# Batch 0's keys and queries in 2 KB runs, two heads stacked on the partitions, and the first batch's steps in another order

## The chip, the core and the metric

The kernel runs on one core of a Trainium2 chip. The metric is the device time of one execution in microseconds. Before the change the median of three runs is 712.56 us (711.0 to 712.8). The engines are called as in the profile: PE (TensorE, matrix products), DVE (VectorE), ACT (ScalarE), POOL (GpSimd) and SP (SyncE, whose instruction stream here only issues DMA transfers). Each engine works through its own instructions in order and waits at an instruction until what it needs is there.

## What is computed

Two attentions, one behind the other, and a gated feed-forward layer on their result. There are 8 batches of 8 heads, 576 tokens and a head size of 64; 32 rows of p attend to all tokens, and then all tokens attend to the 32 packed rows.

```python
def sm_attn(qq, kk, vv):
    s = scale * np.matmul(qq, kk.transpose(0, 1, 3, 2))
    s = s - np.max(s, axis=-1, keepdims=True)
    a = np.exp(s)
    a = a / (np.sum(a, axis=-1, keepdims=True) + 1e-09)
    return np.matmul(a, vv)
p_packed = sm_attn(p, k, v)
out = sm_attn(q, p_packed, p_packed)
...
x = np.ascontiguousarray(attn_out.transpose(0, 2, 1, 3)).reshape(B * S, H * D)
a = x @ w_a
b = x @ w_b
return (a * b @ w_out).astype(np.float32)
```

x has 4608 rows of 512, w_a and w_b are 512 by 1536, w_out is 1536 by 512. All is float32.

## The kernel before

**Stages.** The packed rows of a batch are multiplied into w_a and w_b (the small products g, line 380), so that a batch's feed-forward input is an attention matrix of 576 tokens by 256 (8 heads by 32 packed rows). A first product makes a and b from it (`mm1`, line 398, in float32r halves "hi" and "lo", three products for each pair), DVE multiplies them, and a second product with w_out (line 424 for batch 0, line 738 later) gives the output. Twelve tiles `ft` of 128 columns cover the 1536. Batches 0 and 1 run in this plain form, batches 2 to 7 in a loop of periods with fewer products (line 779), which the change doesn't touch.

**Attention steps.** For a batch, `stage1(b, e)` handles the four heads of one parity e ("head set e"): scores of p against k (line 264), maximum (270), exp (282), transposes (300), product with v (310). `stage2(b, e)` does the second attention: scores (325), transposition out of PSUM (330), maximum (334), subtraction (337), exp (339), sum (343 to 345), multiplication (346), transposition (350), and the halves a2_hi and a2_lo (356, 91). Subtraction and multiplication run on DVE or POOL by the letter in the string SUBS. Each stage is a generator that is moved on by one step whenever its name stands in a list: S0 and S1 start stage 1 for set 0 and 1, r0 and r1 move it on, s0 and s1 move stage 2 on, P turns the packed rows, T turns p, k and q turn tiles of keys and queries, Lk, Lq, Lv and Lp issue loads.

**Weights.** Each block of w_a, w_b and w_out is loaded as two 32-bit words for each number (`raw`, lines 216 and 223). Step A works on the high words (line 195, ACT), B on the low words (ACT line 203, DVE or POOL line 200, by the string WAYS), C combines them into `w_ab` (line 206, DVE); D splits a block of w_out.

**The order by hand.** All five engines run in the order in which the code emits instructions. FIRST is the order of batch 0's loads, all on SP's queue; up to eight transfers are in flight, and the ninth is issued when the first has landed. START is the order of batch 0's attention steps, weight steps and fillers (W, nine products that only keep TensorE going, line 567) until the first feed-forward product. PLAN_0 has a slot for each half tile of batch 0's first product and for each of the first nine f of its second product; its steps belong to batch 1's attention (with their own loads for batches 1 and 2) and to the weights. TURN says which engine copies each transposed tile out of PSUM.

**Batch 0's loads.** `load_first` (line 131) loads k and q each as two transfers of 512 KB, heads 0 to 3 and heads 4 to 7. A partition holds four tokens of each of four heads, in runs of 4 by 64 numbers, 1 KB; a third transfer (128 KB, 32 partitions) brings the last 64 tokens. `turn_first` (line 145) transposes four 128 by 128 blocks for each pair of heads and copies them out of PSUM as one block of 512 columns. `load_v` (line 164) loads v for one head set in one transfer for the first 512 tokens and two small ones for the rest. `store_first` (line 442) writes batch 0's rows back in the token order that the loads set.

Of the kernel before, what the change touches and what calls it, by code (L numbers as in the profile page):

```python
# [8 lines left out]
F32 = mybir.dt.float32  # L9
# [10 lines left out]
def tile_packed_attn_gated_ffn(  # L20
# [20 lines left out]
    nc = tc.nc  # L41
    B, H, S, D = q.shape
# [3 lines left out]
    P = 128  # L46
    R, E = 4, 2
# [24 lines left out]
    scratch = early.__enter__()  # L72
# [3 lines left out]
    ident = const.tile([P, P], F32, name="ident")  # L76
# [28 lines left out]
    nats, xTs = {}, {}  # L105
# [23 lines left out]
    firsts = {}  # L129

    def load_first(src, key, part):

        if part < 2:
            t = scratch.tile([P, R, 4 * D], F32, name=f"{key}n{part}")
            nc.sync.dma_start(
                out=t, in_=src[0, R * part:R * part + R, 0:4 * P, :].rearrange("h (p i) d -> p h (i d)", i=4))
        else:
            t = scratch.tile([P, H, 2 * D], F32, name=f"{key}n{part}")
            nc.sync.dma_start(out=t[0:TR], in_=src[0, :, 4 * P:S, :].rearrange("h (p u) d -> p h (u d)", u=2))
        firsts[key, part] = t  # L140

    def turn_first(key, n):

        if (0, key) not in xTs:
            pool = scratch if key == "q" else ld
            xTs[0, key] = [pool.tile([P, R, HS], F32, name=f"xT{i}") for i in range(2)]
        copy = (nc.vector.tensor_copy, nc.scalar.copy)[int(TURN["kq".index(key) * 5 + n])]
        x = bank_pair()[:, 0, :] if n in (2, 3) else bank()
        if n < 4:
            h = 2 * (n % 2)  # L150
            for i in range(4):
                nc.tensor.transpose(
                    x[:, P * i:P * i + P], firsts[key, n // 2][:, h + i // 2, P * (i % 2):P * (i % 2) + P], ident)
            copy(out=xTs[0, key][n // 2][:, h:h + 2, 0:2 * P], in_=x.rearrange("p (h t) -> p h t", h=2))
# [8 lines left out]
    def load_v(b, e):  # L163


        t = ld.tile([P, R, NT, D], F32, name="vt") if b or e == 0 else scratch.tile([P, R, NT, D], F32, name="vt1")
        vv = v[b].rearrange("(r e) s d -> e s r d", e=E)[e]
        n = 2 if b else 4
        for i in range(4 // n):
            nc.sync.dma_start(  # L170
                out=t[:, :, n * i:n * i + n, :].rearrange("p r u d -> p r (u d)"),
                in_=vv[n * P * i:n * P * i + n * P].rearrange("(p u) r d -> p r u d", u=n).rearrange("p r u d -> p r (u d)"))
        for u in range(2):
            nc.sync.dma_start(
                out=t[TR * u:TR * u + TR, :, 4, :],
                in_=vv[4 * P:S].rearrange("(p u) r d -> u p r d", u=2)[u])
        vts[b, e] = t
# [19 lines left out]
    def low_word(raw, way):  # L197
        low = raw[..., 0]
        if way:
            (nc.vector if way == 1 else nc.gpsimd).tensor_scalar(  # L200
                out=low, in0=low, scalar1=2.0 ** -29, scalar2=7.0, op0=ALU.mult, op1=ALU.min)
        else:
            nc.scalar.activation(out=low, in_=low, func=AF.Copy, scale=0.93 * 2.0 ** -29)
# [115 lines left out]
    def stage2(b, e):  # L319
# [15 lines left out]
        yield  # L335
        eng = nc.vector if b < 2 and SUBS[2 * b + e] == "1" else nc.gpsimd
        eng.tensor_tensor(out=s2, in0=s2, in1=mx.unsqueeze(2).broadcast_to([P, TU, J]), op=ALU.subtract)
# [104 lines left out]
    def store_first(ob, x, i):  # L442

        for u in range(2):
            if x < 8:
                rows = out[0:4 * P].rearrange("(a l i) n -> a i l n", a=4, i=4)[x % 4, 2 * (x // 4) + u]
            else:
                rows = out[4 * P:S].rearrange("(l u) n -> u l n", u=2)[u]
            nc.sync.dma_start(out=rows, in_=ob[i + TL * u:i + TL * u + TL])
# [55 lines left out]

    st = {}

    FIRST = ("k0 p0 k2 k1 q0 v0 q1 v1 q2 w1 w1 w1 w1 w1 w1 w1 w1 w1 w1 w1")
    START = ("T0 k0 k4 k1 k3 k2 q0 S0 S1 r0 r1 q1 r1 r0 r0 r1 r0 q2 r1 q3 q4 P0 s0 B s1 W A s0 B A A s0 s0 B s1 C A s1 B s0 C s1 A s1 C B B Lp2 C A B A s0 s1 B C B B s0 B g A C A A s1 Lk2 C C A A C B B Lk3 C s1")
    WAYS = ("000000022220202120012012011200010010")  # L510
    TURN = ("0001110101")
    SUBS = ("0100")

    PLAN = (" |  |  | S0 | r0 | r0 |  | r0 |  | r0 Lv1 ; S1 | r1 | r1 q0 Lk2 | r1 | r1 | q1 Lk3 Lv2 P0 |  ; s0 | s0 s0 | s0 T2 | "
            "s0 Lp4 | s0 s1 | s1 s1 | s1 | s1 | s1 | t0 t1 t2 t3 u0 | k2 |  | k3 Lq2")
    PLAN = dict(enumerate(PLAN.split("|")))
    PLAN_0 = ("A | C C | B A B A | B C C B C | A A | C | B Lv0 | C B A T0 k0 Lp2 A | A A B B C Lq0 | C C k1 | A B A | S0 B | B A r0 | C C C | B A Lq1 |  | C C B r0 r0 D A A | S1 C D | B C B B A D | r1 C | A A D | r0 T2 |  | q0 B r1 C B D r1 C |  | A | D B C Lv1 A | r1 A B D Lk2 B C B q1 D Lk3 A A P0 | C s0 s0 D C Lp4 A B | s1 s0 | Lv2 | D | s0 s1 s0 | k2 s0 s1 C k3 | s1 |  | Lq2 D s0 s1 s1 Lq3 s1")
    PLAN_0 = dict(enumerate(PLAN_0.split("|")))

    pieces = [(c, n) for c in range(NC) for n in range(4)] + [(NC, f) for f in range(NFT)]  # L520
# [12 lines left out]
    def convert(x):  # L533
# [62 lines left out]
    emit(0, START, tasks)
    drain(tasks["g"])
# [316 lines left out]
    for n in range(LAST):  # L914
        b, ft = NB + n // NFT, n % NFT
# [18 lines left out]
    i, c0 = tiles[-1]  # L934
# [35 lines left out]
```

## Time and profile before

| | us |
|---|---|
| median of three runs | 712.56 |
| lowest and highest run | 711.0, 712.8 |
| span of the profiled execution, first to last instruction | 710.5 |
| TensorE busy in that span | 700.2 |
| DVE, ACT, POOL busy | 452.7, 363.6, 416.2 |
| first product of line 398 starts | 32.29 |

The profiled execution is known by its span alone; the lowest of the timed runs is 0.5 us longer and the median 2.06 us. The granted TensorE clock is 1.000. Times in the trace are counted from the first instruction. A row of the timeline gives start and length in us, engine, line, operation, tiles written and read, size and count, and in brackets how long the engine had been idle before and what ended that. A matrix product in float32 appears as two instructions. In the table by stretches the last two columns are the share of time in which the 16 DMA engines were busy (slightly over 1 when all are) and the GB/s that they moved.

### The profile page before, as it was taken

The page shows a single profiled execution, that of the slowest core. Times are in us where ns is not written, and L with a number is a line of the kernel's source. Part 1 is how long each engine was busy: PE and PEld are TensorE (multiplying, and loading weights), DVE is VectorE, ACT ScalarE, POOL GpSimd, SP SyncE. Part 2 cuts the span into 40 slices and gives each one's busy share as a digit, 9 for nine tenths or more (in the row PEclk, how much of TensorE's full clock was granted, in tenths as well). Part 3 has the DMA queues.
Part 4 walks back from the last instruction along what each step waited for, and adds up shares of the span by engine and source line. Part 5 has one row for each costly group of instructions (what it writes and reads, how often), then busy time and mean ns, then how long its engine had stood idle before and what let it go on. Part 6 is the DMA issues. An engine that isn't in the chain of part 4 may idle for free.

```text
span 710.5 us, 14214 instructions
## 1 busy us (share of the span) xinstructions
PE 700.2 (99%) x5568; PEld 574.8 (81%) x5568; DVE 452.7 (64%) x820; ACT 363.6 (51%) x733; POOL 416.2 (59%) x322
## 2 busy tenths in 40 slices
PE   8899999999999999999999999999999999999998
PEld 6488978898878888878888788788888878888886
DVE  3998655467355679665775678765785667754342
ACT  3878743544254555645554456545555446544510
POOL 0586752327244677746874589556775578856520
PEclk9999999999999999999999999999999999999999
DMA  9999963668254736446433564456145323133002
GB/s 267 385 249 326 235 138 75 184 155 286 78 127 155 180 85 167 127 134 152 137 95 123 155 177 94 118 181 166 60 120 160 104 90 119 60 121 116 1 1 75
DMA packets 178243, 102.64 MB, mean 144 GB/s; under 512 B 142464, under 2 KB 160640, under 8 KB 172800
## 3 DMA queue, kind: packets, MB, share of 16 engines
q1 hardware_dynamic: 178176, 101.73, 50.4%
q8 instruction: 44, 0.72, 0.4%
q14 instruction: 23, 0.19, 0.1%
HBM read 85.98 MB, written 15.73 MB: 143 GB/s over the span
## 4 chain that ended last, share of the span: by engine, by line
PE 94%; DVE 3%; ACT 1%; DMA 1%; issue 0%; SPq 0%; DVEq 0%; ACTq 0%
PE x L738 37%; PE m L779 29%; PE m L398 10%; PE m L424 5%; PE x L793 5%; PE s L310 2%; PE s L325 1%; PE s L264 1%; PE x L380 1%; PE s L300 1%; DMA qn<-in_q_dram 1%; DVE w_ab L206 1%; DVE a_lo L91 0%; PE x L310 0%; ACT raw L195 0%
## 5 line engine op out<-in xcount | busy, mean ns | idle before, releaser
L738 PE MATMUL x<-wo,h_hi 128*128 128x512 f32 (+1 forms) x776 | 249.2, 391 | 0.0
L91 POOL TENSOR_TENSOR h_lo<-asb,h_hi 128x576 fp32r<-128x576 f32 x96 | 140.6, 1466 | 84.5 <-ACT h_hi L824 44.6
L738 PEld LDWEIGHTS x<-wo,h_hi 128*128 128x128 f32 x776 | 140.9, 188 | 22.0 <-ACT gs L799 0.9
L738 PE MATMUL x<-wo,h_lo 128*128 128x512 f32 (+1 forms) x388 | 152.1, 392 | 0.0
L91 POOL TENSOR_TENSOR G_lo<-gs,G_hi 128x640 fp32r<-128x640 f32 x72 | 112.7, 1571 | 30.5 <-ACT G_hi L814 30.2
L738 PEld LDWEIGHTS x<-wo,h_lo 128*128 128x128 f32 x388 | 72.9, 188 | 11.7
L91 POOL TENSOR_TENSOR A_lo<-gs,A_hi 128x256 fp32r<-128x256 f32 x36 | 27.3, 758 | 89.1 <-ACT A_hi L802 89.1
L861 DVE TENSOR_TENSOR d<-m,d 128x576 f32<-128x576 f32 (+1 forms) x73 | 54.1, 741 | 34.7 <-ACT d L857 34.0
L874 DVE TENSOR_TENSOR asb<-m,d 128x288 f32<-128x288 f32 x72 | 32.5, 451 | 66.1 <-ACT c L870 64.2
L870 ACT COPY c<-m 128x288 f32<-128x288 f32 x72 | 28.8, 399 | 79.2 <-PE m L779 79.2
L748 DVE TENSOR_TENSOR part<-x,part 128x512 f32<-128x512 f32 (+1 forms) x65 | 44.1, 679 | 38.8 <-PE x L738 38.8
L779 PE MATMUL m<-tx_hi,G_hi 128*128 128x288 f32 x216 | 63.8, 296 | 0.0
L779 PE MATMUL m<-tx_hi,G_lo 128*128 128x288 f32 x216 | 63.7, 295 | 0.0
L799 ACT COPY gs<-x 128x512 f32<-128x512 f32 x36 | 21.1, 587 | 82.5 <-PE x L793 81.2
L779 PE MATMUL m<-tx_lo,G_hi 128*128 128x288 f32 x216 | 63.3, 293 | 0.0
L814 ACT CAST G_hi<-gs 128x640 fp32r<-128x640 f32 x72 | 52.2, 729 | 15.8 <-POOL gs L808 15.2
L857 ACT COPY d<-m 128x576 f32<-128x576 f32 (+1 forms) x73 | 46.6, 639 | 19.9 <-PE m L779 18.2
L824 ACT CAST h_hi<-asb 128x576 fp32r<-128x576 f32 x72 | 49.0, 680 | 11.5 <-DVE asb L888 11.5
L779 PEld LDWEIGHTS m<-a_hi,G_hi 128*128 128x128 f32 x144 | 27.0, 187 | 31.5 <-issue 17.4
L808 POOL TENSOR_TENSOR gs<-gs 128x512 f32<-128x512 f32 x36 | 46.6, 1294 | 4.1 <-DVE gs L805 3.7
L779 PE MATMUL m<-a_hi,G_hi 128*128 128x288 f32 x144 | 47.0, 326 | 0.0
L398 PE MATMUL m<-a_hi,ghi 128*128 128x288 f32 x192 | 43.2, 307 | 1.6 <-ACT ghi L386 1.5
(174 smaller groups left out, 1550.9 us busy)
## 6 DMA issues: line engine op xcount, KB each, us to landing
wr<-w_kept SPq DMA_DIRECT2D x36, 1024.0 KB, 5.0
nat<-in_k_dram SPq DMA_DIRECT2D x56, 144.0 KB, 5.2
nat<-in_q_dram SPq DMA_DIRECT2D x56, 144.0 KB, 5.4
vt<-in_v_dram SPq DMA_DIRECT2D x28, 256.0 KB, 3.8
out_dram<-part SPq DMA_DIRECT2D x27, 256.0 KB, 2.0
raw<-in_moe_w_a_dram SPq DMA_DIRECT2D x12, 512.0 KB, 8.6
raw<-in_moe_w_b_dram SPq DMA_DIRECT2D x12, 512.0 KB, 8.8
raw<-in_moe_w_out_dram SPq DMA_DIRECT2D x12, 512.0 KB, 7.0
```

What stands on the lines that cost most here:

```text
L91: return eng.tensor_tensor(out=dst, in0=src, in1=hi.bitcast(F32), op=ALU.subtract)
L398: nc.tensor.matmul(out=ps[:, half, 0:HS], lhsT=gt[:, kt, ft % 4, cols], rhs=at[:, kt, HS * half:HS * half + HS], start=(n == 0 and kt == 0 ...
L424: nc.tensor.matmul(out=o[:, cols], lhsT=ht[:, c0:c0 + P], rhs=wt[:, cols], start=(ft == 0 and n == 0), stop=(ft == NFT - 1 and n == 2))
L738: nc.tensor.matmul(out=o[:, cols], lhsT=ht[:, c0:c0 + P], rhs=wt[:, cols], start=(ft == fts[0] and n == 0), stop=end)
L748: nc.vector.tensor_tensor(out=parts[i][:, cols], in0=o[:, cols], in1=parts[i][:, cols], op=ALU.add)
L779: nc.tensor.matmul(out=bank[:, n % 2, 0:HS], lhsT=g, rhs=t, start=(first and i == 0), stop=(i == 2), skip_group_check=True)
L793: nc.tensor.matmul(out=gps[e][J * r:J * r + J, :], lhsT=ppT[rows, 2 * (b % 2), r, :], rhs=w[rows, r, :], start=True, stop=True)
L808: nc.gpsimd.tensor_tensor(out=gs[:, 2:4].rearrange("p a u f -> p a (u f)"), in0=gs[:, 0:2].rearrange("p a u f -> p a (u f)"), in1=s2.unsqu ...
L814: nc.scalar.copy(out=G_hi[:, n % 3], in_=gs[:, 1:6, n % 2])
L824: nc.scalar.copy(out=view(h_hi[ft]), in_=src)
L857: nc.scalar.copy(out=d[:, both], in_=X[:, both, 0:HS])
L861: nc.vector.tensor_tensor(out=d[:, both], in0=V[:, both, 0:HS], in1=d[:, both], op=ALU.add)
```

## The change

**Loads.** k and q of batch 0 are still loaded in two large transfers each, but now heads 2a and 2a+1 lie under each other: even heads on partitions 0 to 63, odd heads on partitions 64 to 127. A partition holds eight tokens of each of four heads, a run of 8 by 64 numbers, 2 KB. Each transfer thus writes 64 partitions, and both are needed before a block can be transposed, since a block of 128 partitions now holds two heads. v must follow the same token order, so its 512 KB transfer becomes two of 256 KB, one for each half of the partitions, still in 1 KB runs. The copies out of PSUM and the store rows follow. The SP queue takes both k transfers first, q before v, and the end of q before q's second half.

**Orders.** START, WAYS, TURN, SUBS and PLAN_0 are new. In SUBS batch 0's head set 1 goes from DVE to POOL.

On SP, the first transfers of the program (kn and qn are the tiles of k and q, vt those of v, raw the weight blocks). Before:

```order
L135 DMA kn_113<-in_k_dram 128x4x256
L182 DMA p_nat<-in_p_dram 128x2x64 x2
L139 DMA kn_118<-in_k_dram 32x8x128
L135 DMA kn_120<-in_k_dram 128x4x256
L135 DMA qn_122<-in_q_dram 128x4x256
L170 DMA vt<-in_v_dram 128x4x256
L174 DMA vt<-in_v_dram 32x4x64 x2
L135 DMA qn_128<-in_q_dram 128x4x256
L170 DMA vt_130<-in_v_dram 128x4x256
L174 DMA vt_130<-in_v_dram 32x4x64 x2
L139 DMA qn_134<-in_q_dram 32x8x128
L216 DMA raw<-in_moe_w_a_dram 128x2x512 x2
```

And now:

```order
L138 DMA kn_113<-in_k_dram 64x4x512 x2
L190 DMA p_nat<-in_p_dram 128x2x64 x2
L141 DMA kn_119<-in_k_dram 32x8x128
L138 DMA qn_121<-in_q_dram 64x4x512
L141 DMA qn_123<-in_q_dram 32x8x128
L138 DMA qn_121<-in_q_dram 64x4x512
L174 DMA vt<-in_v_dram 64x4x256 x2
L182 DMA vt<-in_v_dram 32x4x64 x2
L174 DMA vt_131<-in_v_dram 64x4x256 x2
L182 DMA vt_131<-in_v_dram 32x4x64 x2
L224 DMA raw<-in_moe_w_a_dram 128x2x512 x2
```

All large transfers of k, q and v are 64 partitions wide, and v comes behind all of q.

On DVE, batch 0's second attention (s2_0 and s2_1 are the scores of head sets 0 and 1, raw_136 to raw_142 the first four weight blocks). Before:

```order
L252 COPY ppT_100<-x_343 128x256
L330 STREAM_TRANSPOSE s2_0_377<-s_347 128x576
L334 TENSOR_REDUCE mx_379<-s2_0_377 128x18
L330 STREAM_TRANSPOSE s2_1_387<-m_357 128x576
L334 TENSOR_REDUCE mx_389<-s2_1_387 128x18
L206 SCALAR_TENSOR_TENSOR w_ab_95<-raw_136 128x2x256
L337 TENSOR_TENSOR s2_1_387<-s2_1_387,mx_389 128x576
L343 TENSOR_REDUCE sum2_399<-s2_0_377 128x18
```

And now:

```order
L260 COPY ppT_100<-x_337 128x256
L156 COPY xT1_232<-m_341 128x2x256
L214 SCALAR_TENSOR_TENSOR w_ab_95<-raw_136 128x2x256
L338 STREAM_TRANSPOSE s2_0_385<-s_348 128x576
L342 TENSOR_REDUCE mx_387<-s2_0_385 128x18
L338 STREAM_TRANSPOSE s2_1_393<-m_361 128x576
L342 TENSOR_REDUCE mx_395<-s2_1_393 128x18
L214 SCALAR_TENSOR_TENSOR w_ab_95<-raw_138 128x2x256
L351 TENSOR_REDUCE sum2_403<-s2_0_385 128x18
```

The subtraction of head set 1 has left DVE (the multiplication too, further on), and the first weight combination and a q copy stand ahead of the score transposes.

On PE, in batch 0's second product, batch 1's value product of head set 1 (wo are the blocks of w_out, one for each f). Before:

```order
L424 MATMUL m_1181<-wo_1080,h_hi3_499 128x512 x2
L424 MATMUL m_1181<-wo_1080,h_lo3_500 128x512
L310 MATMUL s_1243<-vt_1225,t2_1169 32x64 x20
L250 MATMUL x_1291<-ident_90,pp_1120 128x128 x2
L424 MATMUL m_1180<-wo_1166,h_hi4_501 128x512 x2
```

And now:

```order
L432 MATMUL m_1182<-wo_1036,h_hi2_497 128x512 x2
L432 MATMUL m_1182<-wo_1036,h_lo2_498 128x512
L318 MATMUL s_1234<-vt_1228,t2_1169 32x64 x20
L432 MATMUL m_1181<-wo_1079,h_hi3_499 128x512 x2
L432 MATMUL m_1181<-wo_1079,h_lo3_500 128x512
```

The value product stands behind f = 2 instead of f = 3, and the turn of the packed rows (line 250, now 258) no longer follows it at once but comes behind f = 3. On SP the load of p for batch 2 (two transfers) now stands ahead of that v load, where before it stood behind the next eight k transfers.

The diff, without the unchanged lines and with the tables cut to a line or two:

```diff
@@ load_first
         if part < 2:
-            t = scratch.tile([P, R, 4 * D], F32, name=f"{key}n{part}")
-            nc.sync.dma_start(
-                out=t, in_=src[0, R * part:R * part + R, 0:4 * P, :].rearrange("h (p i) d -> p h (i d)", i=4))
+            t = firsts.get((key, 0))
+            if t is None:
+                t = firsts[key, 0] = scratch.tile([P, R, 8 * D], F32, name=f"{key}n0")
+            rows = src[0, :, 0:4 * P, :].rearrange("(a g) (p i) d -> g p a (i d)", g=2, i=8)[part]
+            nc.sync.dma_start(out=t[64 * part:64 * part + 64], in_=rows)
@@ turn_first
             for i in range(4):
-                nc.tensor.transpose(
-                    x[:, P * i:P * i + P], firsts[key, n // 2][:, h + i // 2, P * (i % 2):P * (i % 2) + P], ident)
-            copy(out=xTs[0, key][n // 2][:, h:h + 2, 0:2 * P], in_=x.rearrange("p (h t) -> p h t", h=2))
+                j = 4 * (i % 2) + 2 * (i // 2) if key == "k" else 2 * i
+                nc.tensor.transpose(x[:, P * i:P * i + P], firsts[key, 0][:, n, D * j:D * j + P], ident)
+            copy(
+                out=xTs[0, key][n // 2][:, h:h + 2, 0:2 * P].rearrange("p h (i t) -> p h i t", i=4),
+                in_=x.rearrange("p (i h t) -> p h i t", i=4, h=2))
@@ load_v
-        for i in range(4 // n):
+        for g in range(0 if b else 2):
+            nc.sync.dma_start(
+                out=t[64 * g:64 * g + 64, :, 0:4, :].rearrange("p r u d -> p r (u d)"),
+                in_=vv[0:4 * P].rearrange("(p g u) r d -> g p r u d", g=2, u=4)[g].rearrange("p r u d -> p r (u d)"))
+        for i in range(2 if b else 0):
@@ store_first
-                rows = out[0:4 * P].rearrange("(a l i) n -> a i l n", a=4, i=4)[x % 4, 2 * (x // 4) + u]
+                rows = out[0:4 * P].rearrange("(a l i) n -> a i l n", a=2, i=8)[x % 2, 2 * (x // 2) + u]
@@ tables (START and PLAN_0 are new as well)
-    FIRST = ("k0 p0 k2 k1 q0 v0 q1 v1 q2 w1 w1 w1 w1 w1 w1 w1 w1 w1 w1 w1")
+    FIRST = ("k0 k1 p0 k2 q0 q2 q1 v0 v1 w1 w1 w1 w1 w1 w1 w1 w1 w1 w1 w1")
-    WAYS = ("000000022220202120012012011200010010")
-    TURN = ("0001110101")
-    SUBS = ("0100")
+    WAYS = ("020000022220202120012111011200010010")
+    TURN = ("0000101000")
+    SUBS = ("0000")
```

More of the change, by code (lines that the diff above doesn't have):

```diff
@@ L139, in load_first @@
             nc.sync.dma_start(out=t[0:TR], in_=src[0, :, 4 * P:S, :].rearrange("h (p u) d -> p h (u d)", u=2))
-        firsts[key, part] = t
+            firsts[key, part] = t
     def turn_first(key, n):
@@ L506, in tile_packed_attn_gated_ffn @@
     st = {}
-    FIRST = ("k0 p0 k2 k1 q0 v0 q1 v1 q2 w1 w1 w1 w1 w1 w1 w1 w1 w1 w1 w1")
-    START = ("T0 k0 k4 k1 k3 k2 q0 S0 S1 r0 r1 q1 r1 r0 r0 r1 r0 q2 r1 q3 q4 P0 s0 B s1 W A s0 B A A s0 s0 B s1 C A s1 B s0 C s1 A s1 C B B Lp2 C A B A s0 s1 B C B B s0 B g A C A A s1 Lk2 C C A A C B B Lk3 C s1")
-    WAYS = ("000000022220202120012012011200010010")
-    TURN = ("0001110101")
-    SUBS = ("0100")
+    FIRST = ("k0 k1 p0 k2 q0 q2 q1 v0 v1 w1 w1 w1 w1 w1 w1 w1 w1 w1 w1 w1")
+    START = ("k0 k1 k2 T0 k3 k4 S0 r0 S1 q1 r1 q0 q4 r1 r0 r0 q2 r1 r0 r1 P0 q3 A s0 A B B B s1 W C s0 s0 A s0 B s1 s1 A C s1 s0 B C A s1 B C B B Lp2 A s0 B B A s1 C B s0 A s1 g A C A A B C Lk2 C s1 A C Lk3 C B")
+    WAYS = ("020000022220202120012111011200010010")
+    TURN = ("0000101000")
+    SUBS = ("0000")
     PLAN = (" |  |  | S0 | r0 | r0 |  | r0 |  | r0 Lv1 ; S1 | r1 | r1 q0 Lk2 | r1 | r1 | q1 Lk3 Lv2 P0 |  ; s0 | s0 s0 | s0 T2 | "
@@ L516, in tile_packed_attn_gated_ffn @@
     PLAN = dict(enumerate(PLAN.split("|")))
-    PLAN_0 = ("A | C C | B A B A | B C C B C | A A | C | B Lv0 | C B A T0 k0 Lp2 A | A A B B C Lq0 | C C k1 | A B A | S0 B | B A r0 | C C C | B A Lq1 |  | C C B r0 r0 D A A | S1 C D | B C B B A D | r1 C | A A D | r0 T2 |  | q0 B r1 C B D r1 C |  | A | D B C Lv1 A | r1 A B D Lk2 B C B q1 D Lk3 A A P0 | C s0 s0 D C Lp4 A B | s1 s0 | Lv2 | D | s0 s1 s0 | k2 s0 s1 C k3 | s1 |  | Lq2 D s0 s1 s1 Lq3 s1")
+    PLAN_0 = ("A A B | C | B B | A C | B C C B A A | C | C Lv0 | A C B T0 | k0 Lp2 A Lq0 A A B B C | C C k1 | A B A | | S0 B B C A r0 | C C | B A Lq1 | | C C B r0 r0 D A A | S1 C D | B C B B A D | r1 C | A D | A r0 T2 q0 | B | B r1 C D r1 B C | | Lp4 A | D C Lv1 A r1 | A B Lk2 D B C B q1 D Lk3 A A P0 | C s0 s0 D C | A s1 s0 Lv2 | D s0 B s1 s0 | | k2 | s0 s1 C k3 | s1 | | Lq2 D s0 s1 s1 Lq3 s1")
     PLAN_0 = dict(enumerate(PLAN_0.split("|")))
```

## The prediction

> **What bounds the kernel now.** I read the page first, then a table by stretches, then what TensorE waited for, then the head of the trace instruction by instruction. The page:
>
> ```profile
> span 710.5 us, 14214 instructions
> PE 700.2 (99%) x5568; PEld 574.8 (81%) x5568; DVE 452.7 (64%) x820; ACT 363.6 (51%) x733; POOL 416.2 (59%) x322
> ```
>
> TensorE is busy for all but 10 us. Two rows of the table by stretches say where that rest lies (columns: length, then busy time of PE, PEld, DVE, ACT and POOL, granted clock, DMA share, GB/s):
>
> ```profile
> 20.00:40.00 20.00, 17.62 (x103) 9.62 (x93) 19.76 (x31) 16.11 (x29) 13.45 (x8) 1.00 1.06 380
> 40.00:60.00 20.00, 19.89 (x182) 17.27 (x181) 18.65 (x28) 16.55 (x31) 14.08 (x8) 1.00 0.95 250
> ```
>
> From 40 us on TensorE hardly pauses. From 20 to 40 us DVE is the full engine (19.76 of 20) and the DMA queue is full too (1.06). TensorE's waits, whole program:
>
> ```profile
> PE m L398 <- ACT ghi L386: 1.5, 1, 1.5
> PE s L325 <- DVE ppT L252: 0.6, 1, 0.6
> PE x L380 <- DVE w_ab L206: 0.6, 1, 0.6
> PE x L152 <- DMA qn<-in_q_dram: 0.5, 1, 0.5
> PE x L250 <- DVE pp L316: 0.4, 1, 0.4
> ```
>
> All small. But the head holds more than waits: until the first product of the feed-forward part (L398) starts, TensorE does little that counts, and part of it is filler (L567).
>
> ```profile
> 7.98 1.09 PE L152 MATMUL m<-ident,kn 128*128 128x128 f32 x8
> 15.92 0.96 PE L310 MATMUL x<-vt,a1T 128*32 128x64 f32 x40
> 16.81 0.66 PE L152 MATMUL m<-ident,qn 128*128 128x128 f32 x4
> 19.05 0.72 PE L325 MATMUL s<-xT,ppT 64*32 64x288 f32 x16 [0.61 <-DVE ppT L252]
> 20.19 7.99 PE L567 MATMUL m<-kn,ident 128*128 128x512 f32 x18
> 32.29 0.54 PE L398 MATMUL m<-a_hi,ghi 128*128 128x288 f32 x2 [1.48 <-ACT ghi L386]
> ```
>
> So the end moves with two things: when L398 starts (32.29), and stalls of the in-order TensorE after that. Both are touched here.
>
> **The change part by part: the loads.** The k pair, the q pair and the v pairs are now each written to 64 partitions at a time, one half behind the other on one queue. Before, all large loads wrote 128. What the DMA engines move in each form:
>
> ```profile
> 3.00:4.00 1.00, 1.00 (x4) 0.77 (x3) 0.00 (x0) 0.00 (x0) 0.00 (x0) 1.00 1.08 366
> 4.00:5.00 1.00, 1.00 (x4) 0.82 (x3) 0.00 (x0) 0.00 (x0) 0.00 (x0) 1.00 0.82 185
> 17.00:18.00 1.00, 1.00 (x12) 0.80 (x11) 0.72 (x2) 0.00 (x0) 0.00 (x0) 1.00 1.06 391
> 385.00:385.50 0.50, 0.50 (x6) 0.50 (x5) 0.00 (x0) 0.00 (x0) 0.50 (x1) 1.00 0.95 201
> 385.50:386.00 0.50, 0.50 (x6) 0.50 (x5) 0.00 (x0) 0.10 (x1) 0.50 (x1) 1.00 0.99 217
> 389.00:389.50 0.50, 0.50 (x7) 0.50 (x5) 0.00 (x0) 0.34 (x1) 0.00 (x0) 1.00 1.04 393
> out_dram<-part SPq DMA_DIRECT2D x2, 128.0 KB, 2.3
> ```
>
> At 3 us k goes to 128 partitions in 1 KB runs: 366 GB/s. At 17 us weights go to 128 partitions in 2 KB runs: 391. The change's own words point at that pair of rows: 2 KB runs are worth 7%. But at 385 us two stores of 64 partitions each (128 KB, 2 KB runs, one half behind the other) move 201 and 217 GB/s while the engines are 0.95 and 0.99 busy, and at 389 us one store from 128 partitions moves 393. No load of 64 partitions is in this trace, so the new loads lie between 201 and 391 GB/s; I take 210, as the stores have the same shape, run and queue. [...]
>
> ```profile
> L135 SPq DMA_DIRECT2D kn<-in_k_dram x2: 444/448/453, 0.7 to 3.2; - x2
> DMA to landing us min/median/max: 4.0/4.0/4.7
> 6.52 0.69 DVE L154 COPY xT<-x 128x512 f32<-128x512 f32 x1
> 11.03 0.76 DVE L270 TENSOR_REDUCE nmx<-s 128x1 f32<-128x576 f32 x1 [1.23 <-PE s L264]
> ```
>
> The first k load, 512 KB issued at 0.73, landed in 4.0 us: 1.43 at 366 GB/s, so 2.57 are fixed. The new pair, 1,049 KB at 210 GB/s, takes 5.0 and lands at 0.73 + 2.57 + 5.0 = 8.3. Until now the second half was at hand at 7.98 and the first half's work was done by then. Now every transpose needs both halves, so four copies (0.69 each), p's copy (0.4), the first transposes (0.6) and the score products (0.8) follow 8.3: row maxima (L270) at about 12.9 instead of 11.03, **1.9 us later**. That the score products no longer stand behind the first q load (0.5 of wait, 0.6 of work) is counted in that.
>
> Next is v. Ahead of the last v half lie 3,146 KB in half loads (15.0 us at 210) and 459 KB in small pieces (2.5 us at the 185 of the row at 4 us); it lands at 0.73 + 2.57 + 17.5 = 20.8. The product that needs it (L310) ran at 15.92. The first transfer takes over the path here: +4.9. From there to the second scores (L325) it was 3.13 us, of which two groups of q transposes (L152 at 16.81 and the one behind it, some 1.2 us) now stand ahead of the wait or beside other work. Second scores at 20.8 + 1.9 = 22.7 instead of 19.05: **+3.65**.
>
> **The order on DVE.** The stretch from second scores to finished attention was DVE's:
>
> ```profile
> 19.87 0.78 DVE L330 STREAM_TRANSPOSE s<-s 128x576 f32<-128x576 f32 x1 [0.96 <-PE s L325]
> 22.83 0.68 DVE L206 SCALAR_TENSOR_TENSOR w_ab<-raw 128x512 uint32<-128x512 uint32 x1
> 23.43 0.75 DVE L337 TENSOR_TENSOR s<-s,mx 128x576 f32<-128x576 f32 x1
> 27.28 0.76 DVE L346 TENSOR_TENSOR s<-s,sum 128x576 f32<-128x576 f32 x1
> 29.62 1.43 DVE L350 STREAM_TRANSPOSE a2f<-s 128x576 f32<-128x576 f32 x2
> 21.52 1.16 POOL L337 TENSOR_TENSOR s<-s,mx 128x576 f32<-128x576 f32 x1 [20.22 <-DVE mx L334]
> 25.50 1.41 POOL L346 TENSOR_TENSOR s<-s,sum 128x576 f32<-128x576 f32 x1 [2.83 <-DVE sum L345]
> ```
>
> It lasted from 19.87 to 31.05, 11.2 us. Head set 1's subtraction and multiplication go to POOL (two times 0.67 of DVE pitch off, 1.16 and 1.41 on POOL, which is idle there), and one weight combination (0.67) moves ahead of the stretch. That is 2.0 less: 9.2 us. The other end: through POOL the chain of head set 1 is 3.0 (transposes, maxima) + 1.16 + 0.7 + 1.1 + 1.41 + 0.7 = 8.1, so DVE stays the longer. But the combination that moved ahead now waits for the first weight block, behind 20.8 + 1.34 (512 KB at 391) = 22.1, and ACT does its two word steps with the second block's (landing 23.5) between them: ready at about 24.8, done 25.45. The score transposes queued behind it were ready at 23.55. So the stretch runs from 25.45 to 34.65 by the sum of DVE, 33.6 by the chain through POOL; I take 34.05, **3.0 later** than 31.05, and L398 starts near 35.3. The filler ends at 24 + 8 = 32 and costs nothing. Bounds: at 217 GB/s and with no wait for the weight block +1.5; at 201 and with every landing a microsecond later +5.
>
> The remaining edits come to nothing: which engine copies which transposed tile (DVE's four k copies are counted), three weight words on other engines (POOL takes the second block's low word in its idle time), output rows 8 apart rather than 4 (as many stores of as many bytes).
>
> **The order in the second product.** Batch 1's attention is interleaved. Its last value product needs the v load of head set 1:
>
> ```profile
> 82.44 10.96 PE m L424 x48
> 93.40 0.88 PE s L310 x40
> 94.30 0.29 DVE pp L316
> 85.58 0.94 SPq L170 DMA_DIRECT2D vt<-in_v_dram  x2
> 86.57 0.97 SPq L174 DMA_DIRECT2D vt<-in_v_dram  x2
> DMA to landing us min/median/max: 5.5/5.6/5.8
> 100.62 1.20 SPq L182 DMA_DIRECT2D p_nat<-in_p_dram  x2
> ```
>
> The last piece of v was issued at 87.07 and landed 5.5 to 5.8 later, 92.6 to 92.9; the product started at 93.40, 0.65 to spare. Now it stands one f earlier, 12 products of 0.228 or 2.74 us, and the p load (1.20 of SP's time) is issued ahead of v. If SP's queue and TensorE are late by the same 3 us, TensorE stalls 2.74 + 1.20 − 0.65 = 3.3, with all of the second product queued behind. If SP falls behind less than TensorE does, it is 0. SP issues back to back there and its blocks come about 3.4 us later, so I lean to the stall and take **2.3**. The wait on pp (0.4) goes, since 12 products now cover it.
>
> **The sum.** 3.0 + 2.3 − 0.4 = 4.9; 710.5 + 4.9 = 715.4 for the span. The median of the runs, 712.56, is 2.06 above the profiled span, so **717.5 us**.
>
> **The rivals.** (1) The halves are slow, the v product is covered: 3.0 − 0.4 = 2.6, 715.2. For it: SP's order also moved a q load ahead of a weight load. (2) The halves overlap and load like 128 partitions: k lands at 0.73 + 2.57 + 2.7 = 6.0, v well before 15.9, and of DVE's 2.0 some 1.2 reaches L398, since the POOL chain and ACT's extra word steps stand next. With the stall in the second product: −1.2 + 2.3 − 0.4, 713.3. (3) As 2, without it: −1.6, 711.0. (4) The other side: the halves overlap and DVE's 2.0 and the 0.4 at k reach L398 whole, with 0.4 at pp: −2.8, 709.8. It decides where k lands by 6.4, that is above about 340 GB/s for the pair. For 2 to 4 speaks that no load of this form is in the trace; against them the two rows at 385 us.
>
> **How the numbers follow.** A measurement of this kernel tells some 0.3%, 2.1 us. Chances: forecast 0.50 (its own range 715 to 721), rival 1 0.17, rival 2 0.12, rival 3 0.12, rival 4 0.09. Slower by more: the forecast and nearly all of rival 1, 0.66. Within 0.3%: the rest of rival 1, rivals 2 and 3, 0.25. Faster: 0.09. The range, 711.5 to 721.0, leaves out rival 4, part of rival 3 and the top of the forecast (5 at the head and 3.3 later).
>
> **What would show it.** Right: below 230 GB/s with the DMA share near 1 from 3 to 18 us; L270's twin near 13, the value product near 21, the first L398 twin near 35; a wait of TensorE on v near 94. Wrong: k landed by 6.4, 350 GB/s or more from 3 us on, the first feed-forward product before 32.

## The result, and the profile after

The changed kernel takes 718.54 us (median of 6 runs, 718.05 to 719.49), the kernel before 712.12 in the same measurement (6 runs, 711.00 to 713.29): a ratio of 1.0088, with an interval of 1.0074 to 1.0102. It is 6.4 us slower, and the profiled execution shows nearly all of it ahead of the first feed-forward product. Its page begins:

```profile
span 716.3 us, 14214 instructions
PE 704.4 (98%) x5568; PEld 580.0 (81%) x5568; DVE 452.7 (63%) x824; ACT 360.7 (50%) x727; POOL 421.8 (59%) x324
```

The table by stretches of the changed kernel (columns as before: length, busy time of the five engines, granted clock, DMA share, GB/s), over the time in which k, q and v come in:

```profile
4.00:8.00 4.00, 1.18 (x5) 0.66 (x3) 0.00 (x0) 0.00 (x0) 0.00 (x0) 0.97 1.10 202
8.00:12.00 4.00, 3.29 (x16) 3.32 (x17) 1.84 (x3) 0.00 (x0) 0.00 (x0) 0.50 1.15 202
12.00:16.00 4.00, 3.65 (x52) 2.92 (x54) 1.60 (x4) 0.43 (x2) 0.00 (x0) 0.50 1.09 212
16.00:20.00 4.00, 3.90 (x40) 3.32 (x29) 3.00 (x11) 2.31 (x6) 0.00 (x0) 0.75 1.20 221
```

Two things stand there. The DMA engines are full (share above 1) and move 202 to 221 GB/s: the halves load at the rate that the two half stores had (201 and 217), as the forecast's 210 said. And the clock granted to TensorE is 0.50 from 8 to 18 us, which nothing in the profile of before showed (1.00 in its quoted rows). TensorE's timeline:

```profile
8.71 1.94 PE L155 MATMUL x<-ident,kn 128*128 128x128 f32 x8 [3.53 <-DMA kn<-in_k_dram]
20.91 1.73 PE L318 MATMUL x<-vt,a1T 128*32 128x64 f32 x80
24.00 1.14 PE L333 MATMUL s<-xT,ppT 64*32 64x288 f32 x14
24.98 0.41 PE L333 MATMUL s<-xT,ppT 64*32 64x288 f32 x2
33.72 1.78 PE L388 MATMUL x<-w_ab,ppT 64*32 64x512 f32 x16
38.01 0.54 PE L406 MATMUL m<-a_hi,ghi 128*128 128x288 f32 x2 [2.51 <-ACT ghi L394]
39.43 0.68 PE L406 MATMUL m<-a_hi,ghi 128*128 128x288 f32 x2
97.58 0.90 PE L318 MATMUL s<-vt,t 128*32 128x64 f32 x40
```

The first transposes wait 3.53 us for k, the second scores (L333) start at 24.00 instead of 19.05, the first feed-forward product (L406) at 38.01 instead of 32.29: 5.72 later. The value product of batch 1, in the last row, has no wait in front of it. From L406 to the end it is 716.3 − 38.01 = 678.3 us; before, it was 710.5 − 32.29 = 678.2. So what is to be explained is the start of L406. DVE, and then ScalarE, in the stretch ahead of it:

```profile
15.64 0.76 DVE L278 TENSOR_REDUCE nmx<-s 128x1 f32<-128x576 f32 x1 [2.14 <-PE s L272]
26.36 0.69 DVE L214 SCALAR_TENSOR_TENSOR w_ab<-raw 128x512 uint32<-128x512 uint32 x1 [1.71 <-ACT raw L211]
26.97 0.78 DVE L338 STREAM_TRANSPOSE s<-s 128x576 f32<-128x576 f32 x1
35.44 0.78 DVE L358 STREAM_TRANSPOSE a2f<-s 128x576 f32<-128x576 f32 x1 [0.36 <-POOL s L354]
```

```profile
23.74 0.69 ACT L203 ACTIVATE raw<-raw 128x512 f32<-128x512 f32 x1 [1.98 <-DMA raw<-in_moe_w_a_dram]
25.10 0.69 ACT L203 ACTIVATE raw<-raw 128x512 f32<-128x512 f32 x1 [0.67 <-DMA raw<-in_moe_w_a_dram]
36.83 0.66 ACT L203 ACTIVATE raw<-raw 128x512 f32<-128x512 f32 x1
37.39 1.06 ACT L394 CAST ghi<-x 128x512 fp32r<-128x512 f32 x2
```

The chain reads from the loads on: ScalarE waits for the first weight block until 23.74 and for the second until 25.10, DVE waits for the words until 26.36, and only behind that combination stand the transposes of the second scores, whose products for head set 0 had been done by 25.4 (the row at 24.98 in TensorE's timeline). From there DVE's stretch runs without a stop worth naming to 36.22, and ghi follows one word step late.

### The profile page after: what moved, and what is told of

Its sections match the earlier page's. It is cut to its first block, busy times and chain, and to the rows that moved or that the text cites. A ratio compares the mean times of both kernels' runs of the same rounds, so it can differ in the third digit from the quotient of the medians.

```text
span 716.3 us, 14214 instructions
## 1 busy us (share of the span) xinstructions
PE 704.4 (98%) x5568; PEld 580.0 (81%) x5568; DVE 452.7 (63%) x824; ACT 360.7 (50%) x727; POOL 421.8 (59%) x324
## 4 chain that ended last, share of the span: by engine, by line
PE 93%; DMA 3%; ACT 1%; DVE 1%; issue 0%; POOL 0%; SPq 0%; DVEq 0%
PE x L746 37%; PE m L787 29%; PE m L406 10%; PE x L801 5%; PE m L432 5%; PE s L318 2%; DMA vt<-in_v_dram 1%; PE s L333 1%; PE s L272 1%; PE x L388 1%; DMA raw<-in_moe_w_a_dram 1%; DMA kn<-in_k_dram 1%; PE s L308 1%; ACT raw L203 0%; DVE w_ab L214 0%
## 5 line engine op out<-in xcount | busy, mean ns | idle before, releaser
L746 PEld LDWEIGHTS x<-wo,h_hi 128*128 128x128 f32 x776 | 140.9, 188 | 22.1 <-ACT gs L807 1.0
L406 PE MATMUL m<-a_hi,ghi 128*128 128x288 f32 x192 | 43.9, 310 | 2.9 <-ACT ghi L394 2.5
```

Source lines behind the costliest of these rows:

```text
L406: nc.tensor.matmul(out=ps[:, half, 0:HS], lhsT=gt[:, kt, ft % 4, cols], rhs=at[:, kt, HS * half:HS * half + HS], start=(n == 0 and kt == 0 ...
L746: nc.tensor.matmul(out=o[:, cols], lhsT=ht[:, c0:c0 + P], rhs=wt[:, cols], start=(ft == fts[0] and n == 0), stop=end)
```

## The experiments

The theory after the result has two parts. H: 64 partitions at a time load at half the rate, so all that is loaded ahead of the weights takes some 6 us longer. W, for which H is the cause: the first weight words, not k or v, decide when the feed-forward part starts. The rivals: O, the new order of steps costs the time by itself; C, the lowered clock costs it; V, late k and v cost it. All kernels, each with its own time and, from its profile, where the first feed-forward product starts (each ratio is to the kernel before in the same measurement, where that took 711.88 to 712.15):

| kernel | us (median) | ratio to before, interval | span | first feed-forward product | from there to the end |
|---|---|---|---|---|---|
| before | 712.12 | | 710.5 | 32.29 | 678.2 |
| changed | 718.54 | 1.0074 to 1.0102 | 716.3 | 38.01 | 678.3 |
| e1 loads alone | 721.08 | 1.0113 to 1.0147 | 719.3 | 41.42 | 677.9 |
| e2 order alone | 712.82 | 1.0004 to 1.0023 | 710.3 | 32.08 | 678.2 |
| e3 alternating partitions | 713.26 | 1.0010 to 1.0031 | 711.3 | 33.04 | 678.3 |
| e4 two queues | 718.81 | 1.0080 to 1.0109 | 717.0 | 38.04 | 679.0 |
| e5 TensorE kept busy | 718.71 | 1.0084 to 1.0114 | 717.5 | 37.88 | 679.6 |
| e6 = e2 + filler | 713.37 | 1.0012 to 1.0040 | 712.4 | 32.91 | 679.5 |
| e8 combination later | 718.48 | 1.0076 to 1.0102 | 716.9 | 37.66 | 679.2 |
| e9 = e2, two steps later | 713.07 | 1.0003 to 1.0023 | 710.6 | 31.59 | 679.0 |
| e10 v by heads | 736.42 | 1.0324 to 1.0357 | 734.6 | 55.11 | 679.5 |
| e12 = e2, weights late | 719.93 | 1.0092 to 1.0125 | 718.0 | 39.09 | 678.9 |
| e15 mixed | 712.30 | 0.9995 to 1.0014 | 710.4 | 30.93 | 679.5 |

(e11, 768.45 us, is told below.) The last column is within 1.7 us in all of them; the column before it spans 24. The six executions of the changed kernel alone differ by 1.3 us in span (716.3 to 717.6), so a difference of 1 us in one profile says little.

### e1 and e2: the loads alone, the order alone

```diff
 e1: functions of the changed kernel, tables of before
-    FIRST = ("k0 k1 p0 k2 q0 q2 q1 v0 v1 w1 ...")
+    FIRST = ("k0 p0 k2 k1 q0 v0 q1 v1 q2 w1 ...")   (START, WAYS, TURN, SUBS, PLAN_0 too)
 e2: tables of the changed kernel, load_first, turn_first, load_v, store_first of before
```

> Loads, transposes, v and stores of the changed kernel, steps in the order of the kernel before. Theory H (writing 64 partitions at a time at some 210 GB/s makes k, v and the first weights late): 716 to 720 us, +4 to +8 against before, with the DMA rate at 175 to 230 GB/s up to 20 us and the first feed-forward product (L406) at 36 to 40. Rival O (the new order of steps is what costs: the weight combination ahead of the scores' transposes, ScalarE's extra word steps ahead of ghi): 712 to 714, L406 at 32 to 34.

> Steps in the changed kernel's order, with k, q and v loaded to 128 partitions in 1 KB runs and the stores as in the kernel before. Theory H: 709 to 712, at or below before: k whole at 6.4, first feed-forward product (L398) at 29.5 to 32, no drop of TensorE's clock. Rival O: 716 to 718, L398 at 36 to 38, and DVE waiting for the first weight words as in the changed kernel.

Measured: 721.08 and 712.82, the second above the 709 to 712 that H had. The loads alone cost 9.2 us, the order alone 0.9; H holds, O falls. The first feed-forward product of e1 stands at 41.42, later than either theory said, since in the old order k's second half comes behind p and the small k piece, and q's second half behind v. So with the new loads the new order gains 2.5 us (721.08 to 718.54); with the old loads it gains nothing. e2's ScalarE, DVE and TensorE (three views):

```profile
17.74 0.68 ACT L195 ACTIVATE raw<-raw 128x512 f32<-128x512 f32 x1 [1.01 <-DMA raw<-in_moe_w_a_dram]
```

```profile
21.00 0.78 DVE L330 STREAM_TRANSPOSE s<-s 128x576 f32<-128x576 f32 x1
```

```profile
32.08 0.54 PE L398 MATMUL m<-a_hi,ghi 128*128 128x288 f32 x2 [2.30 <-ACT ghi L386]
33.48 0.68 PE L398 MATMUL m<-a_hi,ghi 128*128 128x288 f32 x2
```

The first weight words start at 17.74 there and at 23.74 in the changed kernel: 6.00 apart, the score transposes behind the combination 5.97 (21.00 and 26.97), and the first feed-forward products 5.93. e2 also shows the clock fall (0.68 instead of 0.43 us a pair at 33.48) behind a wait of 2.30 us.

### e3: the same runs, on alternating partitions

```diff
-            nc.sync.dma_start(out=t[64 * part:64 * part + 64], in_=rows)
+            nc.sync.dma_start(out=t[part::2], in_=rows)
 turn_first's copy reads the columns in that order; v in one transfer of 128 partitions, stores as before
```

> The changed kernel with k and q in the same 2 KB runs (8 tokens by 64), but the two heads on alternating partitions (0, 2, 4 ... and 1, 3, 5 ...) instead of stacked, so that a transfer's 64 partitions lie all over the 128; v in one transfer of 128 partitions. Theory H, if what limits a transfer is which partitions it reaches: 340 to 390 GB/s from 3 us on, first feed-forward product at 29.5 to 32, 709 to 712. Theory H, if it is their number (64) alone: 210 GB/s, 715 to 719. Rival O: 716 to 719 at any rate of the loads.

Measured: 713.26 us, first feed-forward product at 33.04. The table by stretches of e3:

```profile
4.00:8.00 4.00, 3.29 (x12) 2.42 (x11) 0.35 (x1) 0.00 (x0) 0.00 (x0) 1.00 1.06 321
8.00:12.00 4.00, 3.65 (x39) 3.29 (x45) 2.76 (x5) 0.43 (x2) 0.00 (x0) 1.00 1.07 314
12.00:16.00 4.00, 3.10 (x65) 2.58 (x44) 2.73 (x7) 2.07 (x5) 0.00 (x0) 1.00 1.12 299
```

314 and 321 GB/s while k and q come in and 299 with v behind them, over stretches that hold the small pieces too (e2 has 305, 316 and 318 there): these transfers of 64 partitions, lying all over the 128, run at the rate of e2's transfers of 128. What lowers the rate in the changed kernel, 202 and 202 GB/s over the two stretches from 4 to 12 us, is which 64 partitions a transfer writes, not that they are 64. Why the rate depends on them no run shows. The 2 KB runs bring nothing that can be seen: e3 lies 0.44 us above e2. It came out above the expected 709 to 712, as e2 did.

### e4: the halves on two queues

```diff
-            nc.sync.dma_start(out=t[64 * part:64 * part + 64], in_=rows)
+            (nc.sync, nc.scalar)[part].dma_start(out=t[64 * part:64 * part + 64], in_=rows)   (v's halves too)
```

> The changed kernel with the second half of each k, q and v pair issued from ScalarE's queue instead of SyncE's, so that both halves may be on their way at once. If the limit is that one half follows the other on one queue: 340 GB/s or more from 3 us on, k whole near 6.5, 713 to 715. [...]

Measured: 718.81 us. The table by stretches of e4:

```profile
4.00:8.00 4.00, 1.82 (x5) 0.92 (x3) 0.00 (x0) 0.88 (x1) 0.00 (x0) 1.00 1.08 233
8.00:12.00 4.00, 1.50 (x12) 1.29 (x12) 1.89 (x3) 0.00 (x0) 0.00 (x0) 1.00 1.12 222
16.00:20.00 4.00, 4.00 (x58) 3.42 (x43) 1.90 (x5) 1.76 (x4) 0.00 (x0) 0.50 1.18 199
```

199 to 233 GB/s: two queues change little, though both halves were on their way at once (the k half on SyncE's queue took 7.5 us to land, the one on ScalarE's 5.3). That one half follows the other on one queue, as the forecast put it, is not the limit.

### e5 and e6: the clock

```diff
 e5: -    def warm_first(n=5):    +    def warm_first(n=13):
 e6 (on e2): START  -... s1 g A C A A ...   +... s1 g w A C A A ...   (w: two filler products)
```

> The changed kernel with 13 instead of 5 products of zeros at the start, so that TensorE is busy until k lands near 8.7 us and its clock isn't lowered from 8 to 18 us. Theory C (the lowered clock in the first 18 us costs some 1.8 us at the end): 716.5 to 717, the second scores (L333) near 22 instead of 24.0 and the first feed-forward product near 36. Rival W (the first weight words end last: DVE's first combination waits for them in any case): 718 to 719, L333 near 22 but L406 at 38 as before.

> e2 (the new order with the loads of before) with two more filler products (1.2 to 1.8 us) behind the first weight products, in the 2.3 us in which TensorE waits for ghi. If that wait is what lowers the clock from 32.4 to 36.2: the first products at 0.43 us a pair instead of 0.68, the same start at 32.1, and 711.4 to 711.8 where e2 took 712.8. If the clock falls for another reason: 712.5 to 713.5.

Measured: 718.71 and 713.37, no gain in either. In e5 the clock no longer fell at 8 us, but at 17.8. Up to there the gain can be seen, in TensorE's timeline and DVE's:

```profile
9.96 1.04 PE L155 MATMUL x<-ident,kn 128*128 128x128 f32 x8
```

```profile
14.31 0.76 DVE L278 TENSOR_REDUCE nmx<-s 128x1 f32<-128x576 f32 x1 [0.90 <-PE s L272]
```

The fillers, now 13, pushed the first transposes back by 1.25 us (9.96 for 8.71), but from them to the row maxima it was 4.35 us instead of 6.93, at 272 ns a transpose instead of 421: the price of the lowered clock on the k chain lies in that difference. Then the clock fell, so the second scores came at 24.18 instead of the 22 that both theories had; DVE waited for the weight words as in the changed kernel:

```profile
26.23 0.69 DVE L214 SCALAR_TENSOR_TENSOR w_ab<-raw 128x512 uint32<-128x512 uint32 x1 [1.40 <-ACT raw L211]
```

So e5 alone doesn't test C: its scores weren't earlier. What speaks against C is the wait in that row and its twin in the changed kernel (1.40 and 1.71 us): the combination stands ahead of the score transposes, and DVE works in order (in the changed kernel the scores of set 0 end at 25.39 and their transposes start at 26.97, behind the combination), so scores that are ready sooner wait for the words. e12, below, loses as much with its transposes and second scores at a recorded clock of 1.00 (2 to 28 us), and e8, whose second scores ran 0.86 us sooner, took the same time (718.48), though its edit changes DVE's stretch too. Of the changed kernel's own six executions, the profiled one had a mean clock of 0.990 and took 718.08; the other five, at 0.997 to 1.000, took 718.05 to 719.49. That the lowered clock costs nothing at all there is not shown. In e6 the clock stayed up (1.00 from 30 to 66 us). TensorE's waits in e6 between 32 and 90 us:

```profile
PE m L398 <- ACT asb L410: 0.8, 2, 0.5
PE m L398 <- ACT ghi L386: 0.6, 1, 0.6
PE m L398 <- DVE asb L413: 0.6, 1, 0.6
```

1.4 us of waits for asb where e2 has 0.4: TensorE ran into ScalarE and DVE, which are still making weights. Its start was 0.8 later than e2's as well, with the first words 0.9 later (18.64), so e6 tells only that the faster clock was not worth its 1.2 us. e2's executions show no gain from it either: the two with a mean clock of 1.000 took 712.88 and 713.05, the other eight, at 0.997 to 0.998, 712.12 to 714.46.

### e8 and e9: the order around the weights

```diff
 e8 (changed kernel) START  -W C s0 s0 A s0 B s1 s1 A C   +W s0 s0 A s0 B s1 s1 C A C
 e9 (on e2): the same, and  -B B A s1 C B s0 A s1 g A C A A   +B B s1 C B s0 s1 g A A A C A A
```

> The changed kernel with one edit: the first weight combination goes back behind the transposes and maxima of the second scores on DVE. If its wait for the first weight words (1.7 us) and its place are what the late loads hit: second transposes at 25.2 instead of 27.0, first feed-forward product 1.2 to 1.8 earlier (36.2 to 36.8), and, since TensorE then waits 1 us instead of 2.5 for ghi, no lowered clock at 38 to 42: 715 to 717. If DVE's sum of work or the weights set the end in any case: 718 to 719.

> e2 (the new order with the loads of before) with two edits of the order: the first weight combination behind the second scores' transposes and maxima, and ScalarE's two high-word steps behind ghi instead of ahead of it. If the two edits are worth what the traces show (0.6 on DVE, 0.6 on ScalarE) and the shorter wait leaves the clock up (1.2): first feed-forward product at 30.8 to 31.0, 710 to 711. If not, 712 to 713.

Measured: 718.48 and 713.07; both expectations of a gain missed. DVE's timeline in e8, GpSimd's and TensorE's:

```profile
24.57 0.78 DVE L338 STREAM_TRANSPOSE s<-s 128x576 f32<-128x576 f32 x1 [0.78 <-PE s L333]
27.53 2.89 DVE L214 SCALAR_TENSOR_TENSOR w_ab<-raw 128x512 uint32<-128x512 uint32 x2
```

```profile
27.14 2.73 POOL L345 TENSOR_TENSOR s<-s,mx 128x576 f32<-128x576 f32 x2
```

```profile
23.14 1.14 PE L333 MATMUL s<-xT,ppT 64*32 64x288 f32 x14
```

The transposes did move, to 24.57 instead of 26.97; 0.86 of these 2.4 us come from the second scores, at 23.14 for 24.00, which the edit didn't touch. But the two combinations, now back to back, took 1.33 and 1.63 us instead of 0.69 and 0.68, with no wait ahead of them: they ran beside GpSimd's two subtractions, which the new order had put on that engine. That is 1.6 of the 2.4 us gone, the first combination itself, now inside the stretch, is 0.6 more, and the first feed-forward product came only 0.35 earlier, at 37.66, with the same wait for ghi (2.51) and the same fall of the clock. e9 shows the like: one of its two combinations took 1.66 beside GpSimd, and the start, expected at 30.8 to 31.0, was 31.59. So e8 doesn't tell whether the place of the first combination costs: a price that neither theory had took its place.

### e10 and e11: 128 partitions, by heads

```diff
 e10: v, one transfer for each of the 4 heads of a set, the two halves as [2][64] partitions
+                in_=vv[0:4 * P].rearrange("(p g u) r d -> g p r u d", g=2, u=4)[:, :, i] ...
 e11: k and q in the same way too, [2][64] partitions in a transfer
```

> The changed kernel with v alone loaded to all 128 partitions at a time (four transfers of 128 KB, one for each head of a set, instead of two halves of 256 KB); k and q as changed. Theory W (what counts is how long all loads ahead of the first weight blocks take, at some 210 GB/s for halves against 350 for whole ones): 1,049 KB go 2.0 us faster, the first weight words (L203) start at 21.7 instead of 23.7, the first feed-forward product (L406) at 36 instead of 38, 716.5. If k alone sets the path (it waits 3.5 us for it): 718 to 719, as the changed kernel.

> The changed kernel with the same layout on chip (two heads stacked, 2 KB runs), but k, q and v each in transfers of all 128 partitions (256 KB each for k and q, 128 KB for v; 16 issues on SyncE instead of 8). Theory W, if a transfer's range of partitions is what halves the rate: 300 GB/s or more from 3 to 16 us, first weight words near 18, first feed-forward product near 32, 712 to 714, like e3. If the stacked layout itself is slow, or SyncE's doubled issues are: 716 to 719.

Measured: 736.42 and 768.45 us, far outside what either theory expected, so neither tells what was asked of it. The tables by stretches of e10 and of e11:

```profile
12.00:16.00 4.00, 3.65 (x52) 2.92 (x54) 1.61 (x4) 0.43 (x2) 0.00 (x0) 0.50 0.71 142
16.00:20.00 4.00, 3.89 (x40) 3.29 (x29) 3.00 (x11) 2.35 (x6) 0.00 (x0) 0.76 0.16 52
```

```profile
4.00:12.00 8.00, 2.91 (x9) 1.63 (x7) 0.69 (x1) 0.00 (x0) 0.00 (x0) 0.84 0.12 45
12.00:20.00 8.00, 1.12 (x4) 0.72 (x4) 0.69 (x1) 0.00 (x0) 0.00 (x0) 0.50 0.20 64
```

A share of 0.12 to 0.20 of 16 engines is that of two to three engines. In these transfers the outermost count is 2 (the halves), in the other loads of the head 32, 64 or 128; they are also half as large as those of the changed kernel and twice as many. Which of this makes them slow no run shows, as none changed one of them alone. The stretches with 0.16 and 0.20 hold small transfers of other shapes too. e10 does serve as a third point for W: its first weight words start at 40.16, 22.4 later than e2's, and its first feed-forward product 23.0 later.

### e12: late weights alone

```diff
-    FIRST = ("k0 k1 p0 k2 q0 q2 q1 v0 v1 w1 w1 ...")
+    FIRST = ("k0 k1 p0 k2 q0 q2 q1 v0 v1 x0 x1 x2 x3 w1 w1 ...")   (x: 512 KB into a part of w_ab not yet in use)
```

> e2 (the new order with the loads of before) with four unused loads of 512 KB (2,097 KB, some 5.8 us at 360 GB/s) between the last v load and the first weight block: k, q and v are as early as in e2, and only the weights are late. What is loaded is never read. Theory W: the first weight words near 23.5, first feed-forward product near 37.5 to 38, 717.5 to 719, so late weights alone give the loss of the changed kernel. Rival V (late k and v set it, and the weights have slack): 713 to 715.

Measured: 719.93 us. Its ScalarE, DVE and TensorE:

```profile
24.84 0.67 ACT L195 ACTIVATE raw<-raw 128x512 f32<-128x512 f32 x1 [8.80 <-DMA raw<-in_moe_w_a_dram]
```

```profile
27.44 0.69 DVE L206 SCALAR_TENSOR_TENSOR w_ab<-raw 128x512 uint32<-128x512 uint32 x1 [7.36 <-ACT raw L203]
```

```profile
39.09 0.85 PE L398 MATMUL m<-a_hi,ghi 128*128 128x288 f32 x2 [1.64 <-ACT ghi L386]
```

k, q and v were early (DVE waits 7.36 us with the second scores long there), and the loss was that of the changed kernel and more: the first words 7.10 later than e2's, the first feed-forward product 7.01 later, the time 7.1 longer. From the first words to that product it is 14.25 to 14.34 us in e2, in the changed kernel, in e5, e6 and e12 alike, and 14.0 to 15.0 in e3, e4, e8 and e10. W holds: in this order of steps the weights have no slack, and late weights alone are enough. V falls in so far as it needs weights with slack. What late k and v would cost with early weights no run shows. An estimate from the rows: the changed kernel's second scores of set 0 end at 25.39, and e2's transposes start at 21.00, so late k and v alone would cost some 4.4 of the 5.9 us. Both delays run side by side; that of the words is the longer by 1.6 (26.97 less 25.39), and the one that counts.

### e15: the version that the runs point to

```diff
 on e2: PLAN_0 of before, and in START
-P0 q3 A s0 A B B B s1 W C ... B B A s1 C B s0 A s1 g A C A A
+P0 q3 A B s0 A B B s1 W C ... B B s1 C B s0 s1 g A A A C A A
```

> The version that the runs point to: loads of before, the new order up to the first feed-forward product, and behind it the order of before (PLAN_0), with two edits: ScalarE makes both words of the first weight block before it turns to the second, and its two high-word steps stand behind ghi. Theory D (in e2, e6 and e9 what was won ahead of the first feed-forward product was given back between 42 and 60 us, where DVE is full and waits for GpSimd's word steps, by the new order of PLAN_0): first feed-forward product at 30.8 to 31.3, no wait of TensorE for asb, 710 to 711.3. If the words bind in either order: 712 to 713.5, with TensorE waiting for asb or w_ab before 60 us.

Measured: 712.30 us, a ratio to before of 0.9995 to 1.0014: no faster than before. TensorE and DVE:

```profile
30.93 0.53 PE L398 MATMUL m<-a_hi,ghi 128*128 128x288 f32 x2 [1.30 <-ACT ghi L386]
```

```profile
38.53 1.75 DVE L206 SCALAR_TENSOR_TENSOR w_ab<-raw 128x512 uint32<-128x512 uint32 x2 [1.23 <-POOL raw L200]
```

The start came as expected, 1.36 earlier than before's and with the clock up (1.00 from 30 to 36 us), and the rest of the program took 1.3 longer. So theory D, which laid the giving back on the new PLAN_0, is not borne out: it happens with the old one too. DVE's waits for GpSimd's word steps (1.23 us in the row) are there in e2, e6, e9 and e15 alike, and not in before; that they are what takes the gain back is argued from the traces and not shown by a run.

## Why the prediction was right or wrong

The time (717.5 against 718.54) and the sign were right, and so was the cause: half loads at some half of the rate (202 to 221 GB/s, where before's rows for 128 partitions have 366 and 391). That the sum came out so close is luck, as two errors nearly cancel: the head was taken 2.7 us too short, and a stall of 2.3 us was counted that is not there.

1. **Rate of the halves, 210 GB/s: right** (202 to 221; e3 and e4 show what it hangs on). k's first transpose ran at 8.71 for 8.3. **The row maxima came at 15.64 for 12.9**, 4.6 later than before where 1.9 was counted. The step that failed: the work behind k was costed with the durations of a TensorE that hadn't paused. After 3.53 us without work its clock was 0.50 from 8 to 18 us, and a transpose took 421 ns for 272. The sum had a wait for k in it, but not what a wait does to the clock. e5, whose clock held over this stretch, took 4.35 us from the first transposes to the row maxima, near the 4.6 of the forecast (8.3 to 12.9); the changed kernel took 6.93.
2. **The value product at 20.8: 20.91, but not for the reason given.** v was to take over the path. TensorE's timeline names no wait for v in front of it; the k chain, late and at half clock, got there at the same time. In e8 the product ran at 20.05, also without a wait for v. Second scores at 24.00 for 22.7.
3. **The first combination waits for the first weight block: right, and it is the step that matters most**; the forecast had it as a part of one term. It was to start at 24.8 and started at 26.36, as the words that ScalarE makes for it began at 23.74 (first block counted as landed at 22.1). That is 1.6. DVE's stretch behind the combination took 9.2 us (27.05 to 36.22), the sum of DVE's work as counted; the forecast had taken 8.6, between that sum and the chain through GpSimd: 0.6. ScalarE's word step ahead of ghi, which the forecast left out, is 0.6 more. Together 5.72 for 3.0, beyond its bound of 5.
4. **The stall on v in the second product: wrong, 0 for 2.3.** SyncE issued that v block from 91.71, 6.1 later than before (85.58); the landing took 4.4 to 5.0 us for 5.5 to 5.8; and TensorE reached the product at 97.58, 4.2 later than before although it stands one step earlier. The case that the prediction named, SyncE falling behind by less than TensorE, is the one that came. It was close: e5 waits 0.28 and 0.27 us for v there. The gain of 0.4 on pp came (before, 0.41 at 94.64).
5. **The filler costs nothing: right.** That the remaining edits come to nothing is not shown one by one. The copies and the weight words are in e2's 0.9 with all the rest of the new tables, where a loss and a gain can hide each other; the output rows 8 apart lie behind L406, where 678.3 stands for 678.2. What no step had: with the clock at 0.50 from 38.5 to 41.9, the first products took 0.68 us a pair for 0.43, about 0.8 us up to the next weight products, and smaller waits came and went, so that all behind L406 nets to 0.1.

The rivals built on full-rate halves (711.0 to 713.3, and 709.8 for the other side) can be read from e2 and e3: 712.8 and 713.3. What they counted on from the new order, 1.2 to 2.4 us ahead of the first feed-forward product, came as 0.2 in e2 (32.08 for 32.29): DVE's stretch is shorter there too, but starts later, as the combination in front of it waits 0.77 us for the words, and ScalarE has its word step ahead of ghi.

## What to carry to other kernels

A load's size and run length don't tell its rate: ask which partitions one transfer writes (with the same sizes and 2 KB runs, k and q came in at 202 GB/s on 64 adjoining partitions and at 314 to 321 on alternating ones) and what its shape is (45 to 64 GB/s in e10 and e11, with an outermost count of 2), and look for another transfer of that shape in the trace, a store if need be. When an early load is slowed, follow everything queued behind it to the last block that an in-order engine will wait for; here the loss is the delay of the first weight words, 6.0 us, almost one to one, while the delay of k and v ran beside it and ended 1.6 us sooner. And a wait put into TensorE's stream can have a second price, its clock (0.50 behind the wait of 3.53 us, and 421 ns a transpose for 272), which need not show in the total where another wait ends later anyway: undo one thing at a time before blaming it.

## What the runs showed of the hardware

- The same 64-partition transfers: 202 to 221 GB/s on partitions 0 to 63 and 64 to 127 (changed, 4 to 20 us), 314 to 321 on alternating ones (e3, 4 to 12 us), 199 to 233 on two queues (e4, 4 to 20 us), all at a DMA share above 1. With an outermost count of 2: 45 to 64 GB/s at a share of 0.12 to 0.20 (e10, 16 to 20 us, and e11, 4 to 20 us).
- The lowered clock came behind single waits of TensorE of 4.42 us (e12), 3.53 and 2.51 (changed), 2.73 (e4, at 12.61), 2.30 (e2), 1.95 (e9) and 1.73 (e3), and not behind 2.56 (e4, at 8.38), 1.48 (before) or 1.30 (e15); in e5 it came at 17.8 us behind several short ones, the longest 1.1. So the length of the last wait doesn't decide it alone; what does is left open. It stayed for 10 us in the changed kernel when transposes and small products followed (3 to 14 in e1, e4 and e5), for 3.4 there when the feed-forward products did (38.5 to 41.9).
- A weight combination on DVE took 0.63 to 0.70 us ahead of the first feed-forward product in the changed kernel and in e2, but 1.33 and 1.63 (e8) and 1.66 (e9) where a subtraction of GpSimd had begun first. Where the combination began first, it kept its 0.68 to 0.70, and the subtraction took 1.54 (changed, at 30.09) and 1.56 (e2, at 24.11) for 1.16. Of four beside GpSimd's word steps (e2, from 33.30) three took 0.68 and one 1.16. So beside the subtractions the one that began second took longer each time in these rows, while beside the word steps most combinations show nothing of it; why, no run shows.
- In e3 the first transposes took 417 ns while the granted clock in the record was 1.00 (4 to 12 us); with a recorded clock of 0.50 they took 421 (changed), with 1.00 otherwise 272 (before, e2, e5). In e8 the first eight took 1.94 us, as in the changed kernel, though the mean clock of that execution was 0.997 for 0.990. So the record doesn't show every stretch in which the products run that slowly.
